# Windowed attention and a gated network in one kernel: where GpSimd's accumulating transfers of the folded weights stand in its queue

## The chip, the core and the metric

The kernel runs on one core of a Trainium2 chip. The metric is the device time of one execution in microseconds (us), as the median of the runs shown; smaller is better. Besides the timed runs there is one profiled execution, whose trace holds every instruction of the five engines: TensorE (PE in the profile, with its weight loads as PEld), VectorE (DVE), ScalarE (ACT), GpSimd (POOL) and SyncE (SP, which here does nothing but issue transfers). Times in the trace count from the start of the span.

## What is computed

Attention over 4 batches of 768 tokens with 8 heads of 64. Each query sees its neighbours at a distance under 16, and one summary for each block of 32 tokens: the elementwise maximum of the block's keys and the mean of its values. The result goes through a gated network with four weight matrices. All arrays are float32.

```python
def attention(q, k, v):                       # B=4, H=8, S=768, D=64
    k_sum = k.reshape(B, H, 24, 32, D).max(axis=3)
    v_sum = v.reshape(B, H, 24, 32, D).mean(axis=3)
    local = scale * q @ k.T                   # kept where |i - j| < 16
    summary = scale * q @ k_sum.T + log(32)
    a = softmax(concat([local, summary]))
    return a @ concat([v, v_sum])

x = attention(q, k, v)                        # 3072 tokens x 512
out = (((x @ w1) * (x @ w2)) @ w3) @ w_out    # w1, w2: 512x1024; w3: 1024x1024; w_out: 1024x512
```

## The kernel before

**Attention.** Two heads make a pair, 512 tokens make a unit, and a step handles one pair of one unit: 6 units times 4 pairs, steps 0 to 23. A step's scores are matrix products (line 353). VectorE adds the mask and takes the maximum (L367), ScalarE the exponentials (L381), VectorE the reciprocal of their sum (L387). The multiply by that reciprocal (L400) stands on one engine per step: the string `NORMALIZE` gives it to GpSimd in steps 1, 3 and 4. Then TensorE transposes the result (L411, into `tp`), ScalarE and VectorE copy it out (L416, L418, L420), and TensorE multiplies it with the values (L431, into `po`), which gives `x`.

**Key sums.** The key tile `k` of a step holds windows of keys with a gap in which the 24 block maxima belong. A maximum is taken by VectorE (L246, `ks`, from a transfer of raw keys, L241); GpSimd copies it into the gap (L340, `gather`, called by `fill`). Scores of a step can't start before the copies of its key sums. GpSimd also copies the value means into the value tile in the first phase (L310).

**The network.** w3 and w_out are first multiplied with each other into a folded weight (`wp0` to `wp7`, matrix products at L123, written out by L227 and L119). Each `wp` tile is 128 x 2 x 512: part 0 is the value rounded to TensorE's float32r format, part 1 what the rounding left. w1 and w2 come in as 1024 KB transfers (`wraw`, L154), and are turned into such pairs by L174, L183, L186, L200 and L119. The first two units go through plain matrix products of these weights (L123); the later four units go through a scheme with fewer products, whose weights are sums and differences of quarters of the plain ones. For that scheme the kernel writes its weights to tensors in device memory ("spills") and reads them again in the second half. `pR` is one such: two tensors that hold `wp` with its two parts added together. Each `wp` tile goes there in two transfers, both in `join_wp` (L872): SP writes part 0 (the plain part, L877), and after it GpSimd issues a transfer that adds part 1 to what is there (`accum_op`, L878). What `pR` holds is read much later, by `sums_of_output` (L896), first at 313.02 us.

**The order of the work.** The first phase is a loop over a counter `t`; the table `WORK` says what is issued at which count. It runs with SP's and TensorE's order as written; the other engines are ordered by a scheduler, by priority. The second phase is one call of `lump(p)` for each step from 8 on. There `MANUAL` (L1195) keeps TensorE's order as written, and a stretch of each lump keeps ScalarE's and VectorE's; GpSimd and SP are left to the scheduler. A lump copies the next step's key sums (`fill(p + 1)`), and then issues the `EXTRA` entries of its number. The eight calls of `join_wp` are `EXTRA` entries of lumps 9 to 12, two in each. The scheduler puts both transfers of each call as early as their inputs allow, so that five of the eight pairs of transfers stand in the first phase, ahead of copies and of a multiply of GpSimd's.

Every engine takes its queue in order. Transfers that GpSimd issues go through a queue of their own (q0 in the profile); SP's go through q1.

Of the kernel before, what the change touches and what calls it, by code (L numbers as in the profile page):

```python
# [11 lines left out]
F32 = mybir.dt.float32  # L12
# [3 lines left out]
ALU = mybir.AluOpType  # L16
# [3 lines left out]
P = 128  # L20
# [50 lines left out]
def attention_moe(ctx, tc, qG, kW, kT, vP, vW, vB, mask, w1, w2, w3T, wo, out, outT):  # L71
    nc = tc.nc
# [14 lines left out]
    NF = w1.shape[0] * FQ // P  # L87
    NJ = w3T.shape[2] // 2 // P
    DO = out.shape[1]
    NK = 7  # L90
    KH = NC // 2
    DH = DO // 2
# [17 lines left out]
    wp = [sb.tile([P, 2, DO], F32R, name=f"wp{i}", tag="wp", bufs=NF) for i in range(NF)]  # L110

    wS = [[tc.dram_tile([P, 2, KH * FQ], F32, name=f"wS{k}_{q}") for q in range(NQ)] for k in range(NK)]
    pS = {k: [tc.dram_tile([P, 2, 2 * DH], F32, name=f"pS{k}_{c}") for c in range(NF // 4)] for k in range(2, NK - 1)}
    pR = [tc.dram_tile([P, 2, 2, 2 * DH], F32, name=f"pR{c}") for c in range(NF // 4)]
    pW = [tc.dram_tile([P, 2, DO], F32, name=f"pW{i}") for i in range(NF)]
    vS = [tc.dram_tile([P, P], F32, name=f"vS{b}") for b in range(B)]

# [510 lines left out]
    def stationary(name, load, to_dram, home, apart=False):  # L628


        if apart:
            t = [[sb.tile([P, 512], F32, name="wr", tag="pt", bufs=6) for _ in range(2)] for _ in range(2)]
        else:
            whole = sb.tile([P, 2, 2, 512], F32, name="wr", tag="ring", bufs=RING)
            t = [[whole[:, i, j] for j in range(2)] for i in range(2)]
        yield from load(t)
        (a11, a12), (a21, a22) = t
        yield 1

        def finished(k, raw):  # L640
            to = sb.tile([P, 2, 512], F32R, name="sp", **home)
            nc.scalar.copy(to[:, 0], raw)
            yield 1
            low(nc.vector, to[:, 1], raw, to[:, 0])
            yield 1
            yield 1
            yield 1
            nc.sync.dma_start(to_dram(k), to.bitcast(F32))
            stored.add((name, k))

        works = []
        nc.vector.tensor_tensor(a22, a21, a22, ALU.add)
        yield 1
        nc.vector.tensor_tensor(a21, a11, a21, ALU.subtract)
        works.append(finished(2, a22))
        next(works[0])
        yield 1
        nc.vector.tensor_tensor(a11, a22, a11, ALU.subtract)
        works.append(finished(5, a21))
        next(works[0])  # L660
        next(works[1])
        yield 1
        nc.vector.tensor_tensor(a12, a12, a11, ALU.subtract)
        yield from staggered([*works, finished(4, a11), finished(3, a12)])
# [202 lines left out]
    def spill_wp(i):  # L867

        n = DO if i >= NF // 2 else DH
        nc.sync.dma_start(pW[i][:, :, :n], wp[i][:, :, :n].bitcast(F32))  # L870

    def join_wp(i):  # L872

        h, c, j = i // (NF // 2), i % (NF // 2) // 2, i % 2
        to = pR[c][:, :, h, j * DH : (j + 1) * DH]
        parts = [wp[i][:, w].bitcast(F32).rearrange("p (i d) -> p i d", d=DH) for w in range(2)]
        nc.sync.dma_start(to, parts[0])  # L877
        nc.gpsimd.dma_start(to, parts[1], accum_op=ALU.add)  # L878

    def sums_of_gates(q):  # L880

# [9 lines left out]
    def sums_of_output(c):  # L891

        def load(t):
            for h in range(2):
                for i in range(2):
                    nc.sync.dma_start(t[i][h], pR[c][:, i, h])  # L896
            yield from range(1, 5)

        return stationary("p%d" % c, load, lambda k: pS[k][c], {"tag": "wp", "bufs": NF}, True)
# [55 lines left out]
    def fetch(s):  # L955
        if s < NS:
            inputs[s] = load_scores(*place(s))
# [5 lines left out]
    def fetch_sums(s):  # L963
        if s < NS:
            load_sums(*place(s), values[s])

    def fill(s):
        if s < NS:
            gather(*place(s), inputs[s][1])
# [85 lines left out]
    def first_keys(p):  # L1055
        raw = kraws.pop(p)
        windows(inputs[p][1], raw)
        summaries(0, p, raw)

    def load_second(k):  # L1060
        second[k] = of_second[k][0]()

    def second_batch(k):
        of_second[k][1](second.pop(k))
# [4 lines left out]
    def means():  # L1069
# [18 lines left out]
    WORK = {  # L1088
        11: [lambda: first_keys(0), lambda: fill(0)],
        13: [means],  # L1090
        17: [lambda: load_second(2), lambda: fetch_sums(0)],
        18: [lambda: first_keys(1), lambda: fill(1)],
        20: [lambda: first_keys(2), lambda: fill(2)],
        21: [lambda: load_second(0), lambda: load_second(1), lambda: fetch(5), lambda: fetch_sums(2)],
        22: [lambda: second_batch(0), lambda: load_second(3), lambda: load_second(4), lambda: first_keys(3), lambda: fetch(4), lambda: fill(3), lambda: fetch_sums(1)],
        23: [lambda: second_batch(1)],
# [21 lines left out]
        WORK.setdefault(46 + 3 * q, []).append(lambda q=q: spill_weights(q))  # L1118
    for i in range(NF):
        WORK.setdefault(48 + i, []).append(lambda i=i: spill_wp(i))  # L1120
    RATE = 8000
    LATER_RATE = 2744

    engines = mybir.EngineType
    with tc.manual_schedule(engines={engines.SP, engines.PE}):
        start_loads(0)
        active, pairs, t = [], [], [-1]
        while units or active or pairs or delayed or WORK or t[0] <= FIRST[-1]:
# [30 lines left out]
            if t[0] < FIRST[NPAIR]:  # L1159
                due = given[0] + RATE  # L1160
            elif t[0] <= NPC:
# [30 lines left out]
    for p in range(2 * NFIRST + 2, NS + 2):  # L1192
        UP_TO[p] = UP_TO[p - 1] + 2.2 * FAST

    MANUAL = {engines.PE}  # L1195
    EXTRA = {
        13: [lambda: moving_x(1, 0), lambda: moving_x(1, 1)],
        14: [lambda: gates_flow(1)],
# [4 lines left out]
    EXTRA.setdefault(18, []).append(lambda: background.append(sums_of_output(1)))  # L1203

    for i in range(NF):
        EXTRA.setdefault(9 + i * 4 // NF, []).append(lambda i=i: join_wp(i))

    def lump(p):

# [35 lines left out]

    with tc.manual_schedule(engines=MANUAL):
        for p in range(NFIRST, NS + 2):
# [70 lines left out]
```

## Time and profile before

| what | value |
| --- | --- |
| time, median of 3 runs | 537.37 us (536.55 to 538.07) |
| the profiled execution's own time | 534.98 us |
| its span, first to last instruction | 533.2 us |
| TensorE busy in the span | 489.5 us (92%) |
| VectorE busy | 364.3 us (68%) |
| ScalarE busy | 315.5 us (59%) |
| GpSimd busy | 51.1 us (10%) |
| moved by transfers | 142.95 MB, mean 268 GB/s |
| mean granted TensorE clock | 0.978 |

How to read the lines shown below: in the timeline and in the chain a row is start, duration, engine, line, operation, and `out<-in`; what stands in square brackets is how long the engine had been idle before, and what ended that. "issue" there means that the engine waited for nothing that the profile can name. In the list of waits a row is total, number, longest. In rows of stretches each engine has its busy time and, in brackets, its instructions; the last three numbers are the granted clock, the mean busy share of the 16 DMA engines, and GB/s. The page's slices are 13.33 us each, with the busy share in tenths.

### The profile page before, as it was taken

How to read it: one execution, taken by the hardware profiler on the slowest of the kernel's cores; microseconds unless marked ns; L12 is line 12 of the kernel's file. 1: busy time of each engine (PE TensorE's matmuls, PEld its weight loads, DVE VectorE, ACT ScalarE, POOL GpSimd, SP SyncE). 2: the span in 40 equal slices, each digit the busy share in tenths (PEclk: the TensorE clock that was granted, in tenths of full speed). 3: DMA queues.
4: the chain of work that ended last, by engine and by line, in shares of the span. 5: the costliest groups of instructions: out<-in, count | busy, mean ns of one | idle time of the engine just before them, and what ended most of it. 6: DMA issues, size and time to landing. Idle time of an engine off the chain costs nothing.

```text
span 533.2 us, 10305 instructions
## 1 busy us (share of the span) xinstructions
PE 489.5 (92%) x3744; PEld 392.2 (74%) x3744; DVE 364.3 (68%) x881; ACT 315.5 (59%) x881; POOL 51.1 (10%) x86
## 2 busy tenths in 40 slices
PE   1989880499999999999999999999999999999996
PEld 0767660488887777777777777878877888888885
DVE  5889962279874386888465878689987308419972
ACT  5587861247735586987799748756985430431720
POOL 1022801520114000000000000000000000000000
PEclk9989996699999999999999999999999999999999
DMA  8995898499969487679978798999867755656652
GB/s 347 412 410 225 292 304 303 91 361 382 403 154 308 149 299 260 212 260 336 379 275 282 258 315 306 371 301 324 258 208 235 241 198 196 197 181 204 202 188 96
DMA packets 55939, 142.95 MB, mean 268 GB/s; under 512 B 5456, under 2 KB 20304, under 8 KB 53328
## 3 DMA queue, kind: packets, MB, share of 16 engines
q1 hardware_dynamic: 52560, 138.09, 73.8%
q0 software_dynamic: 2176, 2.10, 2.8%
q10 hardware_dynamic: 1152, 2.10, 1.0%
q8 instruction: 30, 0.49, 0.4%
q14 instruction: 21, 0.17, 0.1%
HBM read 109.56 MB, written 32.70 MB: 267 GB/s over the span
## 4 chain that ended last, share of the span: by engine, by line
PE 79%; DVE 8%; DMA 6%; ACT 4%; issue 2%; POOL 1%; SPq 0%; POOLq 0%
PE ln L688 44%; PE mm L123 25%; PE po L431 4%; PE sc L353 3%; DMA raw<-in_kT_dram 3%; DVE wf L186 3%; PE tp L411 2%; DVE w L119 2%; ACT sm L381 2%; DMA pR<-wp 1%; DVE wf L183 1%; DMA wraw<-in_wo_dram 1%; DMA v<-in_vW_dram 1%; DVE sm L367 1%; ACT w L200 1%
## 5 line engine op out<-in xcount | busy, mean ns | idle before, releaser
L688 PE MATMUL ln<-xT,ws 128*128 128x512 f32 x672 | 157.3, 393 | 0.0
L688 PEld LDWEIGHTS ln<-xT,ws 128*128 128x128 f32 x672 | 124.9, 188 | 27.9 <-issue 1.0
L123 PE MATMUL mm<-x,w 128*128 128x512 f32 x384 | 91.1, 394 | 0.9 <-ACT x L457 0.8
L123 PEld LDWEIGHTS mm<-x,w 128*128 128x128 f32 x384 | 71.1, 188 | 17.6 <-ACT x L457 0.9
L381 ACT ACTIVATE sm<-sm,mx 128x120 f32<-128x120 f32 x192 | 74.0, 389 | 11.4 <-DVE mx L367 11.3
L688 PE MATMUL ln<-hT,ws 128*128 128x512 f32 x336 | 78.3, 392 | 0.0
L688 PEld LDWEIGHTS ln<-hT,ws 128*128 128x128 f32 x336 | 62.6, 188 | 13.4 <-DVE hT L119 0.2
L708 DVE TENSOR_TENSOR tmp<-ln,tmp 128x512 f32<-128x512 f32 x52 | 35.7, 688 | 52.2 <-PE ln L688 38.1
L123 PE MATMUL mm<-w,w 128*128 128x512 f32 x192 | 52.1, 427 | 14.0 <-ACT w L200 11.9
L606 ACT CAST hT<-hr 128x512 fp32r<-128x512 f32 x56 | 32.0, 621 | 43.4 <-DVE hr L765 35.9
L123 PEld LDWEIGHTS mm<-w,w 128*128 128x128 f32 x192 | 38.1, 204 | 24.9 <-ACT w L200 12.1
L367 DVE CUSTOM_DVE_ANT_0 sm<-sc,mask_sb 128x120 f32<-128x120 f32 x192 | 42.5, 277 | 12.3 <-PE sc L353 12.3
L123 PE MATMUL mm<-wp,h 128*128 128x512 f32 x192 | 46.6, 396 | 0.6 <-ACT o L518 0.6
L123 PEld LDWEIGHTS mm<-wp,h 128*128 128x128 f32 x192 | 35.3, 188 | 9.2 <-ACT o L518 1.2
L391 ACT ACTIVATE sm<-sm,mx 128x120 f32<-128x120 f32 x128 | 38.7, 385 | 4.2 <-DVE mx L387 4.1
L411 PE MATMUL tp<-ident,sm 64*120 64x64 f32 x384 | 17.4, 229 | 22.2 <-POOL sm L400 21.9
L119 DVE TENSOR_TENSOR hT<-hr,hT 128x512 fp32r<-128x512 f32 x56 | 35.7, 687 | 3.1 <-ACT hT L606 3.0
L381 ACT ACTIVATION_READ_ACCUMULATOR sm<-sm,mx 128x1 f32 x192 | 36.7, 191 | 0.0
L411 PEld LDWEIGHTS tp<-ident,sm 64*120 64x120 f32 x384 | 13.8, 138 | 31.1 <-POOL sm L400 22.7
L416 ACT COPY pt<-tp 120x512 f32<-120x512 f32 x24 | 13.8, 578 | 37.5 <-PE tp L411 37.5
L340 POOL COPY k<-ks 128x96 f32<-128x96 f32 (+1 forms) x32 | 11.8, 398 | 205.1 <-DMA k<-in_kW_dram 184.5
L431 PEld LDWEIGHTS po<-pt,v 120*64 120x64 f32 x768 | 24.4, 138 | 9.6 <-issue 7.3
(60 smaller groups left out, 585.6 us busy)
## 6 DMA issues: line engine op xcount, KB each, us to landing
ws<-wS SPq DMA_DIRECT2D x56, 512.0 KB
v<-in_vW_dram SPq DMA_DIRECT2D x24, 512.0 KB
wraw<-in_w3T_dram SPq DMA_DIRECT2D x8, 1024.0 KB
wraw<-in_w_dram SPq DMA_DIRECT2D x8, 1024.0 KB
wS<-sp SPq DMA_DIRECT2D x16, 512.0 KB
ws<-pS SPq DMA_DIRECT2D x16, 512.0 KB
k<-in_kW_dram SPq DMA_DIRECT2D x20, 368.0 KB
raw<-in_kT_dram SPq DMA_DIRECT2D x16, 392.0 KB
```

Of the source, the lines that this page charges most:

```text
L119: eng.tensor_tensor(dst, src, hi.bitcast(F32), ALU.subtract)
L123: nc.tensor.matmul(acc, lhsT=a, rhs=b, start=first and i == 0, stop=last and i == len(terms) - 1)
L186: nc.vector.scalar_tensor_tensor(out=bits[:, some], in0=words[:, some, 0], scalar=29, in1=bits[:, some], op0=ALU.logical_shift_right, op1= ...
L353: nc.tensor.matmul(sc[h][64 * g : 64 * g + 64, i * KR : (i + 1) * KR], lhsT=q[rows, i * P + 64 * g : i * P + 64 * g + 64], rhs=k[rows, i, ...
L367: nc.vector.tensor_tensor_reduce(out=sm[:, j], in0=sc[h][:, i * KR : (i + 1) * KR], in1=mask_sb[:, 0 if blk == 0 else 2 if blk == BLOCKS - ...
L381: nc.scalar.activation(sm[:, j], sm[:, j], AF.Exp, bias=mx[:, 0, j : j + 1], scale=-1.0, accum_out=mx[:, 1, j : j + 1])
L391: nc.scalar.activation(sm[:, j], sm[:, j], AF.Copy, scale=mx[:, 2, j : j + 1])
L411: nc.tensor.transpose(to, p, ident[rows, rows])
L431: nc.tensor.matmul(po[cols, at : at + 64], lhsT=v[:KR, g, i, cols], rhs=pt[g][:, (h * NBLK + i) * 64 : (h * NBLK + i + 1) * 64], start=Tru ...
L606: nc.scalar.copy(dst[0], src)
L688: nc.tensor.matmul(banks[i][:, :U], lhsT=x, rhs=y, start=c + j == 0 and k in o.first, stop=c == steps - 1 and j == 2 and k in o.last, skip ...
L708: nc.vector.tensor_tensor(parts[to], got, parts[more], ALU.add)
```

## The change

`pR`'s layout gets rows of 512 instead of twice 256, so that a `wp` part goes in runs of 2 KB instead of 1 KB, and `sums_of_output` reads it in runs of 1 KB instead of 2 KB. The plain part gets a function of its own, `spill_high`, which the first phase's table issues from SP at counts 58 to 65, behind most of the other spills. `join_wp` keeps GpSimd's accumulating transfer alone, and is an `EXTRA` entry of lumps 8 to 11, two in each. In the second phase GpSimd's order is now kept as written. The bytes of `pR` and the number of transfers are the same.

```diff
-    pR = [tc.dram_tile([P, 2, 2, 2 * DH], F32, name=f"pR{c}") for c in range(NF // 4)]
+    pR = [tc.dram_tile([P, 2, 2, DO], F32, name=f"pR{c}") for c in range(NF // 4)]
...
+    def spill_high(i):
+        nc.sync.dma_start(pR[i % (NF // 2) // 2][:, i // (NF // 2), i % 2], wp[i][:, 0].bitcast(F32))
+
     def join_wp(i):
 
-        h, c, j = i // (NF // 2), i % (NF // 2) // 2, i % 2
-        to = pR[c][:, :, h, j * DH : (j + 1) * DH]
-        parts = [wp[i][:, w].bitcast(F32).rearrange("p (i d) -> p i d", d=DH) for w in range(2)]
-        nc.sync.dma_start(to, parts[0])
-        nc.gpsimd.dma_start(to, parts[1], accum_op=ALU.add)
+
+        to = pR[i % (NF // 2) // 2][:, i // (NF // 2), i % 2]
+        nc.gpsimd.dma_start(to, wp[i][:, 1].bitcast(F32), accum_op=ALU.add)
...
         def load(t):
             for h in range(2):
                 for i in range(2):
-                    nc.sync.dma_start(t[i][h], pR[c][:, i, h])
+                    to = t[i][h].rearrange("p (j d) -> p j d", d=DH)
+                    nc.sync.dma_start(to, pR[c][:, h, :, i * DH : (i + 1) * DH])
             yield from range(1, 5)
...
         WORK.setdefault(48 + i, []).append(lambda i=i: spill_wp(i))
+    for i in range(NF):
+        WORK.setdefault(58 + i, []).append(lambda i=i: spill_high(i))
...
-    MANUAL = {engines.PE}
+    MANUAL = {engines.PE, engines.Pool}
...
     for i in range(NF):
-        EXTRA.setdefault(9 + i * 4 // NF, []).append(lambda i=i: join_wp(i))
+        EXTRA.setdefault(8 + i // 2, []).append(lambda i=i: join_wp(i))
```

GpSimd's queue in the first phase, between the key sums of step 3 and the multiply of step 3 (L400); L340 are copies of key sums, L878 the accumulating transfers, and the two rows with 128x2x24 at the end are copies for steps 4 and 5:

```order
 L326 COPY k<-raw 128x4x64
 L340 COPY k<-ks 128x4x24
-L340 COPY k<-ks 128x2x24
-L878 DMA pR_122<-wp_76 256x1x256
-L878 DMA pR_122<-wp_77 256x1x256
-L878 DMA pR_123<-wp_78 256x1x256
-L878 DMA pR_123<-wp_79 256x1x256
-L878 DMA pR_122<-wp_80 256x1x256
-L340 COPY k<-ks 128x2x24 x2
+L340 COPY k<-ks 128x2x24 x3
 L400 TENSOR_TENSOR sm<-sm,mx 128x960
```

Five accumulating transfers leave this place; the three copies and the multiply follow each other. Nothing else in GpSimd's first phase changes but three more such transfers, which stood behind the multiply of step 4.

GpSimd's queue in the second phase after the change, where eight copies of key sums stood in a row before (steps 8 to 15; the first row here is steps 8 and 9):

```order
L340 COPY k<-ks 128x4x24 x2
L879 DMA pR_122<-wp_76 128x512
L879 DMA pR_122<-wp_77 128x512
L340 COPY k<-ks 128x4x24
L879 DMA pR_123<-wp_78 128x512
L879 DMA pR_123<-wp_79 128x512
L340 COPY k<-ks 128x4x24
L879 DMA pR_122<-wp_80 128x512
L879 DMA pR_122<-wp_81 128x512
L340 COPY k<-ks 128x4x24
L879 DMA pR_123<-wp_82 128x512
L879 DMA pR_123<-wp_83 128x512
```

Two accumulating transfers now stand between the copies of one step and of the next, for steps 10 to 13.

SP's queue at the end of the first phase after the change; L870 is the last of the other spills, L241 raw keys, L303 values, L318 and L320 the queries and keys of steps 8 and 9:

```order
L870 DMA pW_131<-wp_83 128x1024
L873 DMA pR_122<-wp_76 128x512
L873 DMA pR_122<-wp_77 128x512
L873 DMA pR_123<-wp_78 128x512
L873 DMA pR_123<-wp_79 128x512
L873 DMA pR_122<-wp_80 128x512
L241 DMA raw<-in_kT_dram 128x784
L303 DMA v<-in_vW_dram 128x1024 x2
L873 DMA pR_122<-wp_81 128x512
L873 DMA pR_123<-wp_82 128x512
L873 DMA pR_123<-wp_83 128x512
L318 DMA q<-in_qG_dram 128x512
```

Before, five plain parts stood further up, among the loads of the first phase, and the other three stood where the first five stand now, behind both transfers of raw keys; now three of them are ahead of the queries and keys of step 8.

## The prediction

> **What bounds the kernel now.** I began with the page's slices.
>
> ```profile
> PE   1989880499999999999999999999999999999996
> PEclk9989996699999999999999999999999999999999
> ```
>
> From the ninth slice on TensorE is full: nothing in the second half can be shortened by moving GpSimd's work. The hole is slices 7 and 8 (80 to 107 us), where the granted clock falls too. The list of waits, cut to 78 to 101 us, says who is waited for:
>
> ```profile
> POOL pR L878 <- issue: 22.0, 3, 10.2
> PE tp L411 <- POOL sm L400: 21.9, 1, 21.9
> ```
>
> TensorE waits once, 21.9 us, for GpSimd's multiply of step 3; in that time GpSimd itself sits three times ahead of an accumulating transfer. GpSimd's timeline:
>
> ```profile
> 65.42 1.21 POOL L878 DMA_DIRECT2D pR<-wp  x1
> 71.64 1.10 POOL L878 DMA_DIRECT2D pR<-wp  x1 [5.01 <-issue]
> 82.91 1.09 POOL L878 DMA_DIRECT2D pR<-wp  x1 [10.17 <-issue]
> 92.45 1.11 POOL L878 DMA_DIRECT2D pR<-wp  x1 [8.45 <-issue]
> 96.99 1.09 POOL L878 DMA_DIRECT2D pR<-wp  x1 [3.43 <-issue]
> 97.91 2.30 POOL L400 TENSOR_TENSOR sm<-sm,mx 128x960 f32<-128x960 f32 x1
> ```
>
> The five stand 4.5 to 11.3 us apart. For `pR` in 60 to 110 us the trace gives this:
>
> ```profile
> DMA to landing us min/median/max: 4.2/6.0/11.0
> ```
>
> That is the same range, so I read it thus: each accumulating transfer is let go only when the one ahead has landed. So the queue behind the first one stood until 97 us. What else TensorE would have had to wait for, from the timelines at both ends of the hole:
>
> ```profile
> 75.73 2.65 PE L123 MATMUL mm<-w,w 128*128 128x512 f32 x11
> 77.91 0.20 DVE L387 RECIPROCAL mx<-mx 128x8 f32<-128x8 f32 x1 [0.23 <-ACT mx L386]
> 80.38 1.12 ACT L174 ACTIVATE wf<-wraw 128x1024 f32<-128x1024 f32 x1 [2.50 <-DMA wraw<-in_w_dram]
> 81.39 0.58 ACT L227 CAST wp<-mm 128x512 fp32r<-128x512 f32 x1
> 82.14 0.68 DVE L119 TENSOR_TENSOR wp<-mm,wp 128x512 fp32r<-128x512 f32 x1
> 82.74 1.22 DVE L186 SCALAR_TENSOR_TENSOR wf<-wraw,wf 128x1024 uint32<-128x1024 uint32 x1
> 83.87 0.94 DVE L246 TENSOR_REDUCE ks<-raw 128x24 f32<-128x768 f32 x1
> ...
> 100.27 1.11 PE L411 MATMUL tp<-ident,sm 64*120 64x64 f32 x16 [21.88 <-POOL sm L400]
> 101.30 2.86 PE L353 MATMUL sc<-k,q 64*64 64x120 f32 x64
> ```
>
> The reciprocal, the multiply's input, is there at 78.11. The last maxima that the scores of step 5 need are there at 84.81, through a chain in which GpSimd has no part.
>
> **Part 1: the five transfers leave GpSimd's first phase.** The multiply can start at 78.11 instead of 97.91 (the copies ahead of it take maxima that VectorE had made before the reciprocal). Its duration:
>
> ```profile
> L400 POOL TENSOR_TENSOR sm<-sm,mx x3: 1794/2302/2669, 55.7 to 142.3; 128x960 f32<-128x960 f32 x3
> ```
>
> With 2.3 us it ends at 80.4, and the transposes move from 100.27 to 80.4: 19.9 us. TensorE's earlier products end at 78.38, so 2.0 us of waiting are left.
>
> What is late next is the second half of the 64 score products, those of step 5. Latest case: nothing in the chain of maxima moves, they are there at 84.81, the copy on GpSimd takes some 0.25, and 32 products follow at this duration (steps 8, 10 and 13 in the chain of waits, which part 4 needs too):
>
> ```profile
> 176.01 0.98 PE sc L353 x32
> ...
> 201.46 0.98 PE sc L353 x32
> ...
> 236.12 0.98 PE sc L353 x32
> ```
>
> The scores end at 86.05 instead of 104.16 (101.30 + 2.86): a gain of 18.1. Earliest case: the chain hangs on TensorE's own last product, 78.38, then L227, L119, L186 and L246 (0.58 + 0.68 + 1.22 + 0.94), the copy and 32 products: 83.0, a gain of 21.1. Which is nearer depends on the 1024 KB weight transfer behind L174, for which ScalarE waited 2.50 us. Two of the accumulating transfers, of 65.42 and 71.64, and three plain parts (0.79 MB) lay ahead of it or beside it. For `pR` in 60 to 110 us, and for the queues in 65 to 95 us:
>
> ```profile
> L877 SPq DMA_DIRECT2D pR<-wp x3: 525/611/913, 67.7 to 69.0; - x3
> ```
>
> ```profile
> q1 hardware_dynamic: 2400, 7.35, 68.0%
> q0 software_dynamic: 932, 0.91, 21.0%
> ```
>
> q1 moves 7.35 MB in 68% of 30 us, 0.36 MB per us, so the plain parts are 2.2 us; q0 needs 6.3 us for 0.91 MB, 3.5 transfers, so 1.8 us each. SP's own five issues go as well, but the query load behind them waited for TensorE's scores. The weight would land up to 5.8 us sooner; more than the 2.5 us that ScalarE waited can't be had by it. With L174 2.5 us earlier the maxima are there at 82.3 and the scores end at 83.5. I take that: a gain of **20.6**, with 18.1 and 21.1 as bounds.
>
> The clock is in these numbers. Two stretches of 5 us:
>
> ```profile
> 90.00:95.00 5.00, 0.00 (x0) 0.00 (x0) 0.00 (x0) 0.00 (x0) 1.11 (x1) 0.50 0.38 63
> 100.00:105.00 5.00, 4.74 (x110) 4.46 (x112) 2.72 (x3) 2.61 (x3) 4.12 (x8) 0.66 0.21 41
> ```
>
> After the hole TensorE restarts at a granted 0.66, and 64 score products take 2.86 us where twice 0.98 are 1.96; I count them at full clock, since what is left are waits of 2.0 us and about half a us. On this the Trainium skill, TensorE: Matmul & The Clock Gate (Part 1: The HAM clock gate), says that the clock halves after an idle window of about 3.4 us which runs freely. The trace agrees for the long wait (0.50); by the rule a wait of 2 us fills no such window, so the sum would stay as it is, and were the remaining wait as long as a window, the gain would be 0.9 us less.
>
> **Part 2: the loads behind the hole.** By 90 us the loads issued ahead of the hole had landed and the DMA engines were mostly idle until 105 (0.38 busy above, 0.21 in the last row). That pause goes: queries, keys and weights issued when the scores end now queue behind the earlier loads. Those are shortened by part 1's plain and accumulating parts, in all five times 0.26 MB (3.6 us) and five times 1.8 us, 12.6 us of engines' time. The next weight lay, in SP's order, just ahead of these raw keys (start and time to landing, from the chain), and ScalarE took it up in the second row:
>
> ```profile
> 75.68 11.20 DMA raw<-in_kT_dram
> ```
>
> ```profile
> 102.83 1.18 ACT L174 ACTIVATE wf<-wraw 128x1024 f32<-128x1024 f32 x1
> ```
>
> So it landed by 86.9, at most 6.5 us behind the weight of 80.38. With that one 2.5 to 5.8 us sooner, it lands by 81.1 to 84.4. By the shift of 20.6 ScalarE would want it at 82.2. I take 0.3 us lost, with 0 and 2.2 as bounds.
>
> **Part 3: the plain parts at the end of SP's first phase.** Eight issues instead of three there. The first five stand before a wait of SP's for TensorE, and cost nothing. The last three stand ahead of queries and keys of steps 8 and 9: 2.2 us of transfer by the rate above, and three issues. GpSimd's rows there:
>
> ```profile
> 157.10 1.09 POOL L878 DMA_DIRECT2D pR<-wp  x1 [3.68 <-issue]
> ...
> 169.82 0.26 POOL L340 COPY k<-ks 128x96 f32<-128x96 f32 x1
> 171.80 0.26 POOL L340 COPY k<-ks 128x96 f32<-128x96 f32 x1 [1.72 <-DMA k<-in_kW_dram]
> ```
>
> The copy for step 8 ends at 170.1, and its products start at 176.0: 5.9 us of cover, and the accumulating transfer of 157 us and its neighbours no longer compete. Cost nothing; without the cover it would be some 4 us.
>
> **Part 4: accumulating transfers between the copies of steps 9 to 13.** After the copy at 171.8 (all times here before the shift) GpSimd issues eight, two per lump. Let h be the distance at which they are let go: 4.8 us by the row at 157.10, up to 11.3 by those of the first phase. The copy for step 10 stands behind the second, that for step 13 behind the eighth: 172.1 + 7h + 1.1. Its products start at 236.1, so nothing is late up to h = 9.0; the copy for step 10 has until 201.5. Three stretches, two of the first phase and one of the lumps:
>
> ```profile
> 75.00:80.00 5.00, 3.38 (x15) 2.45 (x14) 2.75 (x9) 2.85 (x14) 0.00 (x0) 1.00 1.05 361
> 85.00:90.00 5.00, 0.00 (x0) 0.00 (x0) 0.00 (x0) 0.00 (x0) 0.00 (x0) 0.50 1.06 373
> ```
>
> ```profile
> 206.00:218.00 12.00, 12.00 (x120) 9.31 (x118) 7.06 (x26) 9.21 (x33) 0.27 (x1) 1.00 0.69 248
> ```
>
> The large values of h belong to DMA engines at 1.05, and the lumps have them at 0.69. I take no cost; at h = 11.3 it would be 16 us. SP loads the keys of a later step only when GpSimd's copies have left the buffer, so it is held by the same h and the same cover.
>
> **Part 5: layout and reads.** Runs of 2 KB written and 1 KB read, eight transfers each, the reads in a stretch where TensorE is full. Nothing. Keeping GpSimd's order changes no order among the copies.
>
> **Sum.** 20.6, less 0.3 from part 2, less 0.3 for small shifts in the lumps, is 20.0. From the profiled execution, 534.98, that gives 515.0; it stands 2.4 us under the median of 537.37, so the median would be **517.4**.
>
> **The rivals.**
>
> 1. *The loads become the bound.* Between 90 and 105 us the DMA engines were idle by 0.62 and 0.79 in the two rows of part 1, some 10 of 15 us. If removing the transfers buys none of it back, because they only filled gaps, the weights of the plain gates come that much late: a gain of 10, 527.4. For it: this row after the hole.
>
> ```profile
> 110.00:130.00 20.00, 20.00 (x89) 16.54 (x89) 17.04 (x21) 11.88 (x16) 4.80 (x7) 1.00 1.02 390
> ```
>
> Against it: TensorE is full there even so, and 12.6 us of engines' time go. Chance 0.12.
>
> 2. *Slower: GpSimd's copies come late in steps 10 to 13.* If the accumulating transfers are let go more slowly than h = 9.0, TensorE waits for key sums; at h above 11.8 (7h + 173.2 - 236.1 = 20.0) the loss outweighs the gain, and at 12.5, a tenth above the worst row, it is 24.6 and the time 542. Against it: that worst row belongs to DMA engines at 1.05, and 4.8 us is what the row at 157.10 shows. [...] Chance 0.04.
>
> 3. *Nothing is gained.* Another wait in front of the multiply takes the place of the five: the copies of key sums ahead of it need step 4's keys, which SP issued here:
>
> ```profile
> 70.98 0.61 SPq L320 DMA_DIRECT2D k<-in_kW_dram  x1
> ```
>
> They would have to take 27 us, where the raw keys above took 11.2 in the fullest queue. Time 537. Chance 0.02.
>
> 4. *More than counted.* All of the 21.9 us and the slow restart (0.9): 514.6. It needs the reciprocal 2 us sooner; the maxima ahead of it on VectorE waited so long for raw keys, which part 1 may bring sooner:
>
> ```profile
> 72.36 0.95 DVE L246 TENSOR_REDUCE ks<-raw 128x24 f32<-128x768 f32 x1 [1.98 <-DMA raw<-in_kT_dram]
> ```
>
> Chance 0.05.
>
> **How the numbers follow.** The forecast, a gain of 15.6 to 21.5, has 0.77. Range: the bounds of parts 1 and 2 give 516.3 to 521.8 (gains of 21.1, and of 18.1 - 2.2 - 0.3); it is stretched to 514.0, just past rival 4, and to 524.0, for about half of rival 1, which leaves out rivals 2 and 3 and the rest of 1. About 0.3% (1.6 us) is what a measurement here can tell from no change. Faster 0.94 (forecast, rivals 1 and 4), same 0.02 (rival 3), slower 0.04 (rival 2).
>
> **What would show it.** Right: one wait of `tp` for L400 of 1.5 to 3 us near 80 us, a short one of scores for L340 behind it, the granted clock not at 0.50, no L878 before 140 us, TensorE full from about 85 us, and pairs of L879 some 5 us apart in lumps 8 to 11 with no row of scores waiting for GpSimd. Wrong: a wait for `wraw` or for w's L119 between 82 and 130 us (rival 1); scores waiting for L340 near 180 to 215 us (rival 2).

## The result, and the profile after

The changed kernel takes 518.2 us, the median of six runs (517.22 to 522.89), beside 536.6 us for the kernel before (535.44 to 538.07): a ratio of 0.9676, 95% interval 0.9635 to 0.9718. The forecast was 517.4. The profiled execution is the slowest of the six, 522.89 us (its span is 521.1), where the prediction's sum for it was 515.0, so its trace shows what the change gave and also what some executions lose again.

The slices of the changed kernel, 13.03 us each:

```profile
PE   1889898999999999989999999999999999999996
PEclk9989999999999999989999999999999999999999
```

The hole at slices 7 and 8 is gone; new is an 8 at slice 18 (about 222 to 235 us), with a lower clock. TensorE's timeline and then GpSimd's, at the place of the old hole:

```profile
73.83 5.73 PE L123 MATMUL mm<-w,w 128*128 128x512 f32 x24
79.50 0.68 PE L411 MATMUL tp<-ident,sm 64*120 64x64 f32 x16
80.11 1.46 PE L353 MATMUL sc<-k,q 64*64 64x120 f32 x48
83.96 0.64 PE L353 MATMUL sc<-k,q 64*64 64x120 f32 x16 [2.39 <-POOL k L340]
...
85.61 22.74 PE L123 MATMUL mm<-x,w 128*128 128x512 f32 x99
```

```profile
77.07 1.79 POOL L400 TENSOR_TENSOR sm<-sm,mx 128x960 f32<-128x960 f32 x1
...
83.69 0.22 POOL L340 COPY k<-ks 128x48 f32<-128x48 f32 x1 [0.52 <-DVE ks L246]
```

The multiply L400 runs at 77.07 instead of 97.91 and ends before TensorE has finished its products, so the transposes wait for nothing. What is late next is the maxima for step 5, as forecast, with one wait of 2.39 us. The gates start at 85.61. Before they started here (TensorE's timeline of before):

```profile
105.17 3.01 PE L123 MATMUL mm<-x,w 128*128 128x512 f32 x12
```

That is 19.6 us gained. The later steps give a part of it back. Two rows of TensorE's timeline, the scores of steps 8 and 14, of before and then of after:

```profile
175.94 1.05 PE L353 MATMUL sc<-k,q 64*64 64x120 f32 x32
...
248.13 1.05 PE L353 MATMUL sc<-k,q 64*64 64x120 f32 x32
```

```profile
156.37 1.05 PE L353 MATMUL sc<-k,q 64*64 64x120 f32 x32
...
234.70 1.05 PE L353 MATMUL sc<-k,q 64*64 64x120 f32 x32
```

At step 8 the lead is still 19.6 us, at step 14 it is 13.4: the distance between the two rows has grown from 72.2 to 78.3 us. I use this distance below as the measure of the lumps. Where it grew, the lists of waits of the changed kernel say (160 to 240 us), and the timelines of ScalarE (the first two rows below) and TensorE (the third) show the largest case:

```profile
ACT sp L642 <- DMA wS<-sp: 9.9, 4, 4.6
...
PE mm L123 <- ACT g L490: 2.8, 3, 2.3
```

```profile
216.75 0.62 ACT L642 CAST sp<-wr 128x512 fp32r<-128x512 f32 x1 [4.64 <-DMA wS<-sp]
...
224.96 0.56 ACT L490 COPY g<-mm 128x512 f32<-128x512 f32 x1
```

```profile
225.57 0.96 PE L123 MATMUL mm<-wp,h 128*128 128x512 f32 x3 [2.34 <-ACT g L490]
```

ScalarE makes the weights of the scheme with fewer products (`sp`, L642) in six buffers under the tag "x"; a buffer comes free when its spill to `wS` has landed. ScalarE takes its queue in order, so while it waits 4.64 us for a landing, its later copies wait too, among them `g` (L490), for which TensorE then waits 2.34 us; and in the 5 us behind that wait the granted clock is 0.67 (stretches of 5 us of the same trace):

```profile
225.00:230.00 5.00, 4.43 (x39) 3.61 (x40) 4.96 (x17) 3.27 (x13) 0.35 (x1) 0.67 0.98 333
```

Before, ScalarE's wait for `wS` in 160 to 240 us was 1.9 us in all. New in those lumps are GpSimd's accumulating transfers. They stand there in pairs, and GpSimd is not held between the two:

```profile
154.61 1.92 POOL L879 DMA_DIRECT2D pR<-wp  x2
...
164.51 1.77 POOL L879 DMA_DIRECT2D pR<-wp  x2 [0.17 <-issue]
```

This contradicts a step of the prediction, which read the old trace as "each let go only when the one ahead has landed" and expected the pairs some 5 us apart.

### The profile page after: what moved, and what is told of

It is laid out like the page before. It is cut to its first block, busy times and chain, and to the rows that moved or that the text cites. A ratio compares the mean times of both kernels' runs of the same rounds, so it can differ in the third digit from the quotient of the medians.

```text
span 521.1 us, 10300 instructions
## 1 busy us (share of the span) xinstructions
PE 491.6 (94%) x3744; PEld 392.3 (75%) x3744; DVE 363.2 (70%) x881; ACT 314.9 (60%) x881; POOL 52.3 (10%) x86
## 4 chain that ended last, share of the span: by engine, by line
PE 66%; DVE 13%; DMA 9%; ACT 8%; issue 2%; SPq 0%; POOL 0%; ACTq 0%; DVEq 0%; POOLq 0%
PE ln L688 40%; PE mm L123 19%; DMA wS<-sp 4%; ACT sm L381 3%; PE po L431 3%; DVE wf L186 3%; PE sc L353 2%; DVE w L119 2%; PE tp L411 2%; DMA raw<-in_kT_dram 1%; DMA wr<-pR 1%; DMA wraw<-in_w_dram 1%; DVE wf L183 1%; DVE ks L246 1%; DMA wraw<-in_wo_dram 1%
## 5 line engine op out<-in xcount | busy, mean ns | idle before, releaser
L688 PE MATMUL ln<-hT,ws 128*128 128x512 f32 x336 | 78.3, 392 | 0.0
L688 PEld LDWEIGHTS ln<-hT,ws 128*128 128x128 f32 x336 | 62.6, 188 | 13.4 <-DVE hr L765 0.2
L340 POOL COPY k<-ks 128x96 f32<-128x96 f32 (+1 forms) x32 | 12.4, 400 | 210.4 <-DMA k<-in_kW_dram 156.3
L431 PEld LDWEIGHTS po<-pt,v 120*64 120x64 f32 x768 | 25.7, 143 | 9.6 <-issue 6.7
L200 ACT CAST w<-wf 128x1024 fp32r<-128x1024 f32 (+1 forms) x22 | 21.3, 968 | 15.6 <-DVE wf L186 15.5
L431 PE MATMUL po<-pt,v 120*64 120x64 f32 x768 | 29.1, 231 | 1.7 <-DVE pt L420 1.6
L119 DVE TENSOR_TENSOR sp<-wr,sp 128x512 fp32r<-128x512 f32 x24 | 16.5, 689 | 19.3 <-ACT sp L642 19.3
```

What stands on the lines that cost most here:

```text
L119: eng.tensor_tensor(dst, src, hi.bitcast(F32), ALU.subtract)
L200: nc.scalar.copy(t[:, 0, some], f[:, some])
L340: nc.gpsimd.tensor_copy(k[:, blocks, CUT : CUT + NB], ks[b, p].unsqueeze(1).broadcast_to([P, n, NB]))
L431: nc.tensor.matmul(po[cols, at : at + 64], lhsT=v[:KR, g, i, cols], rhs=pt[g][:, (h * NBLK + i) * 64 : (h * NBLK + i + 1) * 64], start=Tru ...
L688: nc.tensor.matmul(banks[i][:, :U], lhsT=x, rhs=y, start=c + j == 0 and k in o.first, stop=c == steps - 1 and j == 2 and k in o.last, skip ...
```

## The experiments

Two questions, then. Why is GpSimd not held any more: because of the place of the transfers, or because of the layout? And is it the accumulating transfers that delay the spills in the lumps (theory 1), or only that all loads come 20 us sooner and denser (theory 2)? This table holds all runs; the distance is that of the scores of steps 8 and 14, the wait is ScalarE's for `wS` between 160 and 240 us, both in the profiled execution. (In e10 the distance also holds the slow clock behind a hole just ahead of step 8.)

| kernel | median, us (lowest to highest, runs) | ratio to before, 95% | distance, us | wait, us |
| --- | --- | --- | --- | --- |
| before | 536.6 (535.4 to 538.1, 6) | | 72.2 | 1.9 |
| changed | 518.2 (517.2 to 522.9, 6) | 0.9635 to 0.9718 | 78.3 | 9.9 |
| e1_after_again | 521.3 (518.5 to 521.8, 5) | 0.9685 to 0.9734 | 78.0 | 10.7 |
| e2_no_accumulate | 514.3 (514.0 to 518.0, 4) | 0.9582 to 0.9643 | 72.1 | 1.8 |
| e3_layout_only | 522.5 (520.5 to 523.7, 4) | 0.9720 to 0.9772 | 72.5 | 2.2 |
| e4_1kb_in_lumps | 520.4 (517.8 to 524.9, 4) | 0.9675 to 0.9762 | 77.6 | 9.3 |
| e5_add_in_sbuf | 519.1 (515.5 to 520.6, 6) | 0.9639 to 0.9694 | 72.6 | 2.6 |
| e6_later_lumps | 520.9 (518.0 to 523.7, 4) | 0.9674 to 0.9743 | 74.1 | 3.6 |
| e7_scheduler_orders_gpsimd | 515.0 (513.5 to 516.1, 4) | 0.9578 to 0.9617 | 72.7 | 5.8 |
| e8_plain_from_gpsimd | 516.9 (515.7 to 519.9, 5) | 0.9620 to 0.9655 | 72.6 | 2.6 |
| e9_scheduler_orders_again | 513.9 (513.5 to 513.9, 4) | 0.9559 to 0.9597 | 72.3 | 2.4 |
| e10_1kb_scheduler_orders | 534.2 (532.8 to 536.2, 10) | 0.9943 to 0.9983 | 74.3 | 1.7 |
| e11_add_in_sbuf_again | 517.4 (516.3 to 518.5, 2) | 0.9570 to 0.9726 | 76.0 | 6.0 |

### Again, unedited: e1_after_again

> The changed kernel once more, unedited, for a second profile and a ratio. Both theories: 517 to 519 us, a ratio of about 0.967. Theory 1 (the accumulating transfers slow the transfers of lumps 8 to 11, and ScalarE's copies sp wait for the landing of the spills wS): a run near 517.5 shows the same kind of stalls as the profiled one of 522.9, only smaller: TensorE idle by 1 to 2 us between 180 and 240 us where the profiled one was idle by some 4, and scores of step 10 start 19.6 us earlier than before, those of step 14 by 17 to 18. Theory 2 (the pulled-forward loads, whatever the accumulates do): the loss is the same in each execution, about 3 us, at the same places.

The run came out at 521.26, not 517 to 519, so the changed kernel's executions spread over 517 to 523 us. Its trace shows the same loss in the same lumps, and not a smaller one. It can't tell the theories apart.

### Without the accumulating transfers: e2_no_accumulate

```diff
-        EXTRA.setdefault(8 + i // 2, []).append(lambda i=i: join_wp(i))
+        pass
```

> The changed kernel without the eight accumulating transfers; left out of the computation is the addition of the second half of wp to pR. Theory 1 (these transfers slow their neighbours in lumps 8 to 11): what was given back between steps 10 and 14 comes back, the scores of step 14 stand as much earlier than before as those of step 10 (19.6 us), TensorE waits under 0.5 us between 180 and 240 us, and the time is 514 to 516 us. Theory 2 (the pause of the DMA engines is lost and the same loads come 20 us denser): the time stays at 517 to 518.5 us and ScalarE still waits for wS in the lumps.

514.25 us, in the range of theory 1, and a distance of 72.1, like before. The stretch of 160 to 240 us of the changed kernel, and then of this one:

```profile
160.00:240.00 80.00, 75.12 (x710) 58.21 (x705) 59.07 (x183) 61.04 (x208) 7.68 (x12) 0.98 0.88 275
```

```profile
160.00:240.00 80.00, 78.69 (x766) 61.58 (x765) 60.09 (x190) 64.21 (x217) 1.82 (x6) 1.00 0.78 262
```

TensorE is busy 3.6 us more, the DMA engines less, and ScalarE's wait is at 1.8 us. Theory 2 falls: the loads come as early here. Theory 1 holds as far as "taking the transfers out of these lumps takes the loss away".

### The same bytes, not adding: e8_plain_from_gpsimd

```diff
+    pX = [tc.dram_tile([P, DO], F32, name=f"pX{i}") for i in range(NF)]
...
-        to = pR[i % (NF // 2) // 2][:, i // (NF // 2), i % 2]
-        nc.gpsimd.dma_start(to, wp[i][:, 1].bitcast(F32), accum_op=ALU.add)
+        nc.gpsimd.dma_start(pX[i], wp[i][:, 1].bitcast(F32))
```

> The changed kernel with GpSimd's eight transfers writing plainly to a scratch tensor instead of adding; left out of the computation is the addition of the second half of wp to pR. The same bytes, places and queue, without reading and adding. If the accumulation is what is costly (q0 took 14.2% of 100 us for 2.10 MB, 1.8 us per transfer, where q1 moves 0.36 MB per us, 0.7 us for 0.26 MB): 514 to 516 us and a share of q0 of 1.1% or less over the span. If any eight transfers more there do it: 517.5 to 521 us as with the adding ones.

516.88 us, just above the range for "the accumulation is what is costly", but below the other one; distance and wait are near those of e2. GpSimd's queue and, under it, the queue of ScalarE's transfers of the output, in the page of the changed kernel, and then GpSimd's queue in the page of this one:

```profile
q0 software_dynamic: 1152, 2.10, 3.0%
q10 hardware_dynamic: 1152, 2.10, 1.1%
```

```profile
q0 software_dynamic: 640, 2.10, 1.0%
```

3.0% of 521.1 us are 15.6 us of all 16 DMA engines, 1.95 each; without adding it is 0.65 each. The edit changes a second thing: the rows of `pX` lie one behind the other, and the same bytes go in 640 packets instead of 1152. The row of q10 sets this aside: plain transfers of as many bytes in as many packets as the accumulating ones take 1.1%. So an accumulating transfer takes nearly three times as long on the DMA engines as a plain one of its size, and part of the loss goes with the adding. The 2.6 us that are left over e2 aren't split further by these runs.

### Adding in SBUF: e5_add_in_sbuf and e11_add_in_sbuf_again

```diff
-        nc.gpsimd.dma_start(to, wp[i][:, 1].bitcast(F32), accum_op=ALU.add)
+        t = sb.tile([P, 2, DO], F32, name="wsum", tag="wf", bufs=5)
+        hi, lo = (wp[i][:, w].bitcast(F32) for w in range(2))
+        nc.gpsimd.tensor_tensor(t[:, 0], hi, lo, ALU.add)
+        nc.sync.dma_start(pR[i % (NF // 2) // 2][:, i // (NF // 2), i % 2], t[:, 0])
...
-    for i in range(NF):
-        WORK.setdefault(58 + i, []).append(lambda i=i: spill_high(i))
```

> The changed kernel with the addition taken out of the DMA queues: at the places of the eight accumulating transfers GpSimd adds the two parts of wp in SBUF (128x512, some 1.0 to 1.4 us each by its 128x960 multiply of 1.79 to 2.67 us), and SyncE spills the sum once, with no plain part before it. If the accumulating transfers are what slows lumps 8 to 11 (theory 1): no TensorE wait between 180 and 240 us and 514 to 515.5 us, as without the addition (514.25), faster than both kernels. If GpSimd's longer hold or a spill that waits for it in SyncE's queue costs as much (rival): scores wait for key sums or loads in the lumps, and 517 us or more.

> The kernel of e5_add_in_sbuf once more for a second profile, since its profile (516.97 us, scores of step 14 start 72.6 us behind those of step 8, as before) shows nothing of what its slower runs (up to 520.63 us) lose. If the lumps are the place: the same distance is 74 to 77 us and a wait of TensorE in 180 to 240 us says for whom. If the first phase is the place (the slow clock behind the short wait of scores): gates start at 86 us or later and the distance stays at 72.2 to 72.7 us.

The median missed: 519.12 instead of 514 to 515.5. The first profile (516.97 us) shows no stall at all; the second one (518.49 us) caught one. From its list of waits, 160 to 240 us, and its TensorE timeline:

```profile
ACT sp L642 <- DMA wS<-sp: 6.0, 3, 4.1
```

```profile
222.51 1.65 PE L123 MATMUL mm<-wp,h 128*128 128x512 f32 x3 [2.18 <-ACT g L490]
```

It is the same chain at the same place, with no accumulating transfer in the kernel. So theory 1 was too narrow: a `wS` spill can land late with no accumulating transfer near. The eight plain spills that SyncE now issues in these lumps are the likely cause, but that is not shown. With the accumulating transfers the stall came in both profiles of the changed kernel, with the plain spills in one of two.

### Later lumps: e6_later_lumps

```diff
-        EXTRA.setdefault(8 + i // 2, []).append(lambda i=i: join_wp(i))
+        EXTRA.setdefault(12 + i // 2, []).append(lambda i=i: join_wp(i))
```

> The changed kernel with the accumulating transfers in lumps 12 to 15 instead of 8 to 11, two each. If their cost comes from meeting the spills and loads of lumps 8 to 13 (theory 1): ScalarE's wait for wS is back to about 2 us there, and 514 to 516.5 us, unless the transfers of lumps 12 to 15 are held up the same way. If they cost the same wherever they stand (rival: 8 times 1.8 us of all DMA engines have to be paid): 517.5 to 521 us, with the waits moved to 220 to 290 us.

520.85 us, which only the rival allows. The wait in the first lumps falls to 3.6 us, and the distance to 74.1, but the median is no better than the changed kernel's. Part of the loss has moved behind the distance: from the scores of step 14 to the end of the span it is 288.2 us here and 285.1 to 286.7 in every other profile, and there ScalarE's longest wait for a spill is 3.52 us, where in e9 it is 1.7 (ScalarE's timeline of e6):

```profile
269.55 0.62 ACT L642 CAST sp<-wr 128x512 fp32r<-128x512 f32 x1 [3.52 <-DMA wS<-sp]
```

This profile is of the fastest of the four runs, so where the slower ones lose more isn't shown; a later place is no better one, that much is.

### The scheduler's order on GpSimd: e7_scheduler_orders_gpsimd, e9_scheduler_orders_again

```diff
-    MANUAL = {engines.PE, engines.Pool}
+    MANUAL = {engines.PE}
```

> The changed kernel without GpSimd in the list of engines that keep source order: five of the accumulating transfers move in front of the copies of steps 7 and 8, behind the multiply of about 121 us, the other three follow those copies; the layout and the plain parts stay. If two or three of the 2 KB transfers at a time go out without GpSimd being held, and 125 to 150 us is where the DMA engines have room (theory 1): no row of scores waits for GpSimd, ScalarE's wait for wS falls to about 4 us, and 514.5 to 517.5 us. If five in a row hold GpSimd (rival), the copies of key sums for steps 8 to 10 come late by 5 us or more: 519 to 525 us.

> The kernel of e7_scheduler_orders_gpsimd once more, unedited, in more runs, since 515.04 us (513.45 to 516.08) would make it the fastest kernel that computes everything. If that stands: 513.5 to 516.5 us, a ratio of 0.958 to 0.962, and below every run of the changed kernel (517.2 and more). If it was chance: 517 us or more.

515.04 and 513.88 us, the fastest kernel here that computes everything, and each of its eight runs is below the changed kernel's fastest, 517.22. GpSimd's timeline of e7:

```profile
119.34 1.79 POOL L400 TENSOR_TENSOR sm<-sm,mx 128x960 f32<-128x960 f32 x1 [15.77 <-DVE mx L387]
126.74 2.82 POOL L879 DMA_DIRECT2D pR<-wp  x3 [5.61 <-DMA pR<-wp]
133.10 0.88 POOL L879 DMA_DIRECT2D pR<-wp  x1 [3.54 <-issue]
135.33 0.87 POOL L879 DMA_DIRECT2D pR<-wp  x1 [1.35 <-issue]
144.48 4.68 POOL L310 COPY v<-vs 24x256 f32<-24x256 f32 x8 [8.28 <-DMA v<-in_vW_dram]
149.11 2.65 POOL L879 DMA_DIRECT2D pR<-wp  x3
```

Three go out at once, the fourth waits 3.54 us. ("DMA pR<-wp" ahead of the first is the landing of a plain part, to which it adds.) For the first of the three (a window around 126.74) the trace gives this:

```profile
DMA to landing us min/median/max: 6.1/6.1/6.1
```

It landed at 132.84, and the fourth starts at 133.10. All eight are issued by 152 us, before the lumps whose spills they delayed; the distance is 72.7 and 72.3. So the new order of GpSimd, kept as written, is itself what costs the changed kernel 3 to 7 us, by the medians of these two against its own two; at the same mean granted clock of 0.999, which one run of the changed kernel and all of e9's have, it is 3.3 us (517.22 against 513.88). In e7 ScalarE still waits 5.8 us for `wS`, with no such transfer left to issue, but in portions of which only 0.3 us reaches TensorE.

### The layout: e3_layout_only, e4_1kb_in_lumps, e10_1kb_scheduler_orders

e3 is the kernel before with this edit; e4 is the changed kernel, and e10 the kernel of e7, with its reverse. The views that write and read `pR` are changed to match:

```diff
-    pR = [tc.dram_tile([P, 2, 2, 2 * DH], F32, name=f"pR{c}") for c in range(NF // 4)]
+    pR = [tc.dram_tile([P, 2, 2, DO], F32, name=f"pR{c}") for c in range(NF // 4)]
```

> The kernel before with only the layout of pR changed (runs of 2 KB written instead of 1 KB); the accumulating transfers stay in GpSimd's first phase, ahead of the multiply of step 3. My prediction's reading (an accumulating transfer is let go only when the one ahead has landed): the five still stand 4.5 to 11 us apart, the multiply starts at 95 to 98 us, the wait of tp is 20 us or more, and the time is 535 to 538 us. The rival (half as many packets go out without being held, as the pairs in the lumps of the changed kernel did, 1.8 us apart): the multiply starts before 83 us, the wait is under 4 us, and the time is 517 to 521 us, so that the layout alone gives the gain.

522.53 us, which is 1.5 above the rival's range and far below my reading's. My reading is refuted: with the transfers left at the old place, and only their runs twice as long and half as many, GpSimd is held once there, and for the landing of a plain part (GpSimd's timeline of e3):

```profile
65.44 1.88 POOL L876 DMA_DIRECT2D pR<-wp  x2
76.62 2.66 POOL L876 DMA_DIRECT2D pR<-wp  x3 [9.29 <-DMA pR<-wp]
...
80.08 1.79 POOL L400 TENSOR_TENSOR sm<-sm,mx 128x960 f32<-128x960 f32 x1
```

The layout alone brings some 13.5 us of the 18. It is 1 to 4 us short of the changed kernel: here TensorE waits 2.34 us for L400 and 4.35 for the maxima, and starts the gates at 91.70 instead of 85.61, but it loses nothing in the lumps (a distance of 72.5).

> The changed kernel with the layout of before (runs of 1 KB) and all else as changed. If the layout decides whether GpSimd is held: the second transfer of each pair in lumps 8 to 11 starts 4.5 to 11 us behind the first, GpSimd's copies of key sums come that much later, which their cover hides up to 9 us, and the time is 517 to 521 us. If it is the place and not the layout: pairs 1.7 to 2 us apart as in the changed kernel, and 517 to 518.5 us.

520.36 us, and the transfers are held 5.6 to 9.1 us apart, as expected of the layout (GpSimd's timeline of e4, first four rows of L882, the same instruction):

```profile
153.28 1.23 POOL L882 DMA_DIRECT2D pR<-wp  x1
158.87 1.11 POOL L882 DMA_DIRECT2D pR<-wp  x1 [4.36 <-issue]
...
165.40 1.09 POOL L882 DMA_DIRECT2D pR<-wp  x1 [3.93 <-issue]
171.86 1.10 POOL L882 DMA_DIRECT2D pR<-wp  x1 [5.37 <-DMA q<-in_qG_dram]
```

No row of scores waits for GpSimd there. From the first transfer to the eighth it is 53.6 us (153.28 to 206.89), 7.7 each on average, under the 9.0 of the prediction's part 4. So in the lumps the cover that the prediction counted is real, and the layout changes nothing that these runs can tell.

> The kernel of e7_scheduler_orders_gpsimd with the layout of before (runs of 1 KB). Theory: GpSimd's queue holds three transfers of 128 rows but only one of 256 (in the runs so far the fourth 2 KB transfer started 0.3 us after the first had landed, each 1 KB one 0.3 us after the one ahead). Then the five behind the multiply of about 120 us go one by one, 4.5 to 6 us apart from 127 us on, the last at 147 to 150; the three that stand ahead of the copies of key sums for steps 8 and 9 are 4.5 to 11 us apart, so that these copies, needed at 156, come at 165 to 175, and TensorE waits 8 to 18 us for k: 524 to 534 us, the hole of before at a later place. If the layout is without effect here (rival): 513.5 to 517 us as with 2 KB.

534.22 us, at the upper end of what was expected (524 to 534): nearly the whole gain is gone again, by the layout alone. GpSimd's timeline, the last four rows of L882, and TensorE's:

```profile
156.48 1.09 POOL L882 DMA_DIRECT2D pR<-wp  x1 [8.16 <-DMA wS<-sp]
...
161.28 1.10 POOL L882 DMA_DIRECT2D pR<-wp  x1 [0.21 <-issue]
165.81 1.09 POOL L882 DMA_DIRECT2D pR<-wp  x1 [3.42 <-issue]
170.37 1.10 POOL L882 DMA_DIRECT2D pR<-wp  x1 [3.47 <-issue]
171.51 0.47 POOL L340 COPY k<-ks 128x96 f32<-128x96 f32 x2
```

```profile
171.83 1.88 PE L353 MATMUL sc<-k,q 64*64 64x120 f32 x32 [18.09 <-POOL k L340]
```

It is the hole of before at another place, and the prediction's rival 2, the late copies, come true in a kernel where their cover is thinner: here the last transfer stands directly ahead of the copy that the scores need.

## Why the prediction was right, and where it was not

**Part 1** was right in mechanism and in size. The multiply was free when the transfers left; the maxima of step 5 were next; scores ended at 84.60 (83.96 + 0.64), 1.1 later than the 83.5 taken and inside the bounds of 83.0 to 86.05. Gates came 19.6 us sooner where 20.6 was forecast. The 1 us between them was lost ahead of the hole. TensorE's scores of step 3, before and after:

```profile
69.00 1.05 PE L353 MATMUL sc<-k,q 64*64 64x120 f32 x32
```

```profile
70.17 1.05 PE L353 MATMUL sc<-k,q 64*64 64x120 f32 x32
```

From there to the gates it is 36.17 us before and 15.44 after, 20.7 less. What set these scores back differs between executions and not between kernels (last section). The wait of `tp` that was to remain (1.5 to 3 us) did not: L400 started at 77.07, not 78.11, and took 1.79 us, not 2.3, and TensorE's own products ended at 79.56, not 78.38. The earlier reciprocal is rival 4's condition in part, without its gain, since the maxima came next.

**Part 2**: no loss where 0.3 was taken. From the gates' start to the scores of step 8 it is 70.77 us before (175.94 - 105.17) and 70.76 after (156.37 - 85.61). Rival 1 did not happen.

**Part 3** was right: in the changed kernel no scores wait for L340 after the one near 84 us.

**Part 4** is the step that failed. It forecast "no cost" because it asked only whether GpSimd's own copies would be late. They are not, even when held (e4). It did not ask what the transfers do to others in the same DMA engines: 1.95 us of all 16 for each, in lumps where ScalarE waits for spills to land. In the profiled executions of the changed kernel this costs 5.8 to 6.1 us of the distance, by the medians of e2 against the two of the changed kernel 4 to 7 us, and between the runs of both with a mean clock of 0.999 some 3 us (517.22 against 513.98 to 514.34). That the median still fell next to the forecast is in part luck: two errors cancel. Without this cost the kernel takes 514.25 (e2), 3.1 us under the forecast. Of these 3.1, 0.8 are the step from the profiled execution to the median, taken as 2.4 us from three runs where the six runs give 1.6, and 0.6 are the losses taken for part 2 and for small shifts in the lumps, which did not come (part 2 above, and e2's distance); the rest stays open. The profiled execution, for which the sum was made, was 7.9 us over it.

**Part 5**, "nothing" for the layout, is right beside the move (e4 against the changed kernel) and wrong by itself. Under it lies a wrong reading: what lets go is not always the landing of the transfer just ahead; all these runs fit with room for a number of rows. In before, each transfer of 256 rows did start when the one ahead had landed, but three of 128 rows go together, the fourth starts when the first has landed, and the fifth when the second has (e7; the second was issued at 127.5 and took 7.6 us, and the fifth starts at 135.33). That a limit of rows or descriptors in flight, at least 384 and under 512, is behind it is inferred from these two cases; nothing here shows it directly.

**The slower rival**, copies late behind held transfers, was rightly given little for this kernel (0.04), since it needed distances above 9 us, seven times over; e10 shows what it does where there is less cover.

## What to carry to other kernels

A transfer that is moved off a queue's critical place still lands somewhere: look there for engines that wait for landings in order, not only for the engine that issues it. Before moving a transfer that holds its queue, try its shape: half as many rows of twice the length removed most of the hold at the old place. And where a scheduler would have chosen another place, measure both.

## What the runs showed of the hardware that was not expected

**Short waits and the clock.** I counted the scores behind a wait of 2 us at full clock, with a rule of the Trainium skill beside it, TensorE: Matmul & The Clock Gate (Part 1: The HAM clock gate). In the changed kernel and in all experiments but e3 and e10 the one wait for L340 there is 2.2 to 3.0 us. In the changed kernel (2.39 us) the 16 products behind it took 0.64 us, as they did in e5 behind 2.98 us; in e2 they took more, at a lower clock (TensorE's timeline, and a stretch):

```profile
83.29 1.08 PE L353 MATMUL sc<-k,q 64*64 64x120 f32 x16 [2.71 <-POOL k L340]
```

```profile
85.00:90.00 5.00, 5.00 (x34) 4.13 (x33) 2.17 (x4) 1.63 (x2) 1.86 (x4) 0.56 0.93 344
```

That execution took 518.03 us where its three others took 513.98 to 514.34. So a wait shorter than the window of about 3.4 us in that rule can lower the clock, and whether it does differs between executions; e1 and e8 show it too, the others with such a wait do not. Shorter waits do so too. TensorE's timeline of the changed kernel, and then of e9, at two places ahead of everything that the two kernels do differently:

```profile
34.79 9.81 PE L123 MATMUL mm<-w,w 128*128 128x512 f32 x35 [1.38 <-DVE w L119]
...
62.71 1.67 PE L431 MATMUL po<-pt,v 120*64 120x64 f32 x28 [1.60 <-DVE pt L420]
```

```profile
34.81 8.21 PE L123 MATMUL mm<-w,w 128*128 128x512 f32 x35 [1.37 <-DVE w L119]
...
61.77 1.03 PE L431 MATMUL po<-pt,v 120*64 120x64 f32 x28 [1.60 <-DVE pt L420]
```

Behind equal waits of 1.4 and of 1.6 us the granted clock, over the 5 us from 34 and from 62 us, is 0.66 in the first kernel's profile and 1.00 in the second's. Over the thirteen profiles the first place is slow in six, the one of before among them, and the second in five. So these kernels spread for two reasons at least: the clock behind short waits, and the stall in the lumps. How the two share the spread stays open; the clock alone doesn't order the runs (two of e1 with 0.996 took 518.54 and 521.62 us).

**The price of adding.** An accumulating transfer of 256 KB took 1.95 us of all 16 DMA engines' time, a plain one from the same queue 0.65 (e8), and a plain one with as many packets, in the changed kernel's q10, 0.72 (1.1% of 521.1 us, for eight).
